# Capped attention and a gated two-layer block: the mix of keys through the PSUM bank of the values, and another order of a step

## The chip, the cores and the metric

The kernel runs on one core of a Trainium2 chip. The metric is the device time of one execution in microseconds (us). Engines are named as in the profile: PE (TensorE, matmuls), PEld (its weight loads), DVE (VectorE), ACT (ScalarE), POOL (GpSimd), SP (SyncE, which here only issues DMAs).

## The reference, cut to what matters

Batch 8, 12 heads, 448 positions, 64 channels a head. The attention's output, heads side by side (768 channels), goes into a block that mixes each position with the one before it.

```python
scores = cap * tanh(scale * q @ k.T / cap)
attn = exp(scores - max) / (sum(exp(scores - max)) + 1e-9)
x = attn @ v                      # heads side by side: 768 channels
xk = mu_k * x + (1 - mu_k) * x_prev     # x_prev: the position before, 0 at the first
xr = mu_r * x + (1 - mu_r) * x_prev
k = relu(xk @ w_k) ** 2                 # 768 -> 1024
out = sigmoid(xr @ w_r) * (k @ w_v)     # 768 -> 768
```

## The kernel before, in words

The first stage of the program walks over 48 pairs of heads (8 batches of 6 pairs; a pair fills the 128 partitions). Everything is kept transposed: scores have keys on partitions and queries along the free axis. A pair's scores come in four blocks of keys, S0 to S3 (`scores`, L182, the last of half size), each with three matmul passes on a high and a low part of q and k, so that the single-pass 32-bit format keeps its accuracy. ACT takes each block through tanh (L197) and exp (L207). PE multiplies the result by the values (`values`, V in the step, L216) into one PSUM bank, `pv`; the pool of these banks has two, used by turns, so that the value group two pairs later needs the bank again. DVE reduces each block's columns (`red`, L225), a DMA gathers the partial sums (`gather`, L230, tile `sq`), DVE adds and inverts them (`recip`, L234 to L238), and the reciprocals go out to DRAM (`rec_store`, L241) and come back spread over all partitions (`rec_load`, L246, tile `r`, one buffer, two DMAs).

`norm` (L250, DVE) multiplies the bank `pv` by `r` into the tile `X`, whose column 0 is zero, so that columns 0 to 447 are the previous positions and 1 to 448 the current ones. `mix_old` (L259, ACT) writes (1 - mu_k) times the previous positions, `mix_new` (L263, DVE) adds mu_k times the current ones in one instruction with two tensor inputs; `xk` (one buffer) is the result. POOL splits it into a high part (`x_high`, L70) and a low part (`x_low`, L80). POOL makes the same split of q and k for a later pair (`qk_high`, L70, and `qk_low`, L80). `x_store` (L275) writes X to DRAM for the second stage. The matmuls of the keys (K in the step, `kpart`, L298) run seven steps behind, 24 a step, into one of two banks; `relu` (L305, ACT) empties a bank and frees it, `k_store` (L311) sends it to DRAM from ACT's queue. Weights arrive as 64-bit numbers: one tile a step (two in some) is converted by five DVE instructions, the `f` entries (L357 to L365), with help of ACT (`weight_abs`, L337) and POOL (`weight_sum`, L372); the last of these instructions starts at 462.6 us.

The order of the instructions is written by hand in the string STEP (L47 to L49), and nothing reorders it: each engine, and SP's queue of DMAs, runs its own instructions in this order. In step i the loads are for pair i + 3, the q and k split for i + 2, scores, tanh, exp and red for pair i, V, gather, recip, rec_store and rec_load for i - 1, and norm, mix_old, mix_new, the split of xk and x_store for i - 2. A digit behind an entry is the block.

After the 48 pairs come seven steps of keys' matmuls alone, in which the converted weights of the second stage are loaded and split; and then the second stage: 28 chunks of 128 positions with the matmuls of L441.

Of the kernel before, what the change touches and what calls it, by code (L numbers as in the profile page):

```python
# [9 lines left out]
F32 = mybir.dt.float32  # L10
F32R = mybir.dt.float32r
AF = mybir.ActivationFunctionType
ALU = mybir.AluOpType
# [3 lines left out]
B, H, S, D = 8, 12, 448, 64  # L17
# [8 lines left out]
P = 128  # L26
# [17 lines left out]

STEP = """gather load_v weight_load more weight_low S0 S1 V S2 f f f f f weight_rest tanh0 exp0 red0 norm  # L47
weight_sum tanh1 recip rec_store exp1 red1 mix_old mix_new K qk_high qk_low x_high x_low tanh2 relu k_store
K exp2 red2 relu k_store S3 K K tanh3 exp3 red3 relu k_store weight_abs rec_load load_qk x_store weight_store"""  # L49


def f(ap):
# [3 lines left out]
class Body:  # L56
# [190 lines left out]
        self.R[i] = r  # L247

    def norm(self, i):
        self.nc.vector.tensor_mul(self.X[i % 2][:, 1:], self.PV.pop(i)[:, 0:S], self.R.pop(i))  # L250

    def mix_old(self, i):
        b, hp = i // NP, i % NP
        if hp == 0:
            xh = self.xkp[b % 2].tile([P, ND, S], F32R, name="xkh", tag="xkh")
            xl = self.xkp[b % 2].tile([P, ND, S], F32R, name="xkl", tag="xkl")
            self.XK[b] = (xh, xl)
        self.xk = self.up.tile([P, S], F32, name="xk", bufs=1)
        self.nc.scalar.mul(self.xk, self.X[i % 2][:, 0:S], self.om["k"][:, hp:hp + 1])  # L259

    def mix_new(self, i):
        hp = i % NP
        self.nc.vector.scalar_tensor_tensor(out=self.xk, in0=self.X[i % 2][:, 1:], scalar=self.mu["k"][:, hp:hp + 1],  # L263
                                            in1=self.xk, op0=ALU.mult, op1=ALU.add)

    def x_high(self, i, e="p"):
        self.copy(e, self.XK[i // NP][0][:, i % NP, :], self.xk)
# [193 lines left out]
    def step(self, i, KS):  # L461
# [6 lines left out]
        pair.update(dict.fromkeys("norm mix_old mix_new x_high x_low x_store".split(), i - 2))  # L468
        for op in STEP.split():
            j = pair.get(op)  # L470
# [180 lines left out]
```

## Time and profile before, and how to read it

| | us |
|---|---|
| runs of the kernel before | 1011.4, 1012.74 (median), 1013.64 |
| the profiled execution, its own time | 1016.09 |
| its span, first to last instruction | 1014.3 |
| PE busy in the span | 967.1 (95%) |
| DVE busy | 667.6 (66%) |
| ACT busy | 500.3 (49%) |
| POOL busy | 297.6 (29%) |

[...] A line such as `L263 DVE SCALAR_TENSOR_TENSOR xk<-x,mu_k,xk ... x48 | busy, mean` is one group: source line, engine, operation, tile written and tiles read, shapes, count, busy time in us, mean in ns, and behind the second bar the idle time of the engine before these instructions and what ended it. In the list of waits, `A <- B` means that A's engine stood idle until B was done. The chain follows the end of the program back from releaser to releaser. `SPq` and `ACTq` are the instruction queues of SP and ACT, in which DMAs are issued.

### The profile page before, as it was taken

The page shows a single profiled execution, that of the slowest core. Times are in us where ns is not written, and L with a number is a line of the kernel's source. Part 1 is how long each engine was busy: PE and PEld are TensorE (multiplying, and loading weights), DVE is VectorE, ACT ScalarE, POOL GpSimd, SP SyncE. Part 2 cuts the span into 40 slices and gives each one's busy share as a digit, 9 for nine tenths or more (in the row PEclk, how much of TensorE's full clock was granted, in tenths as well). Part 3 has the DMA queues.
Part 4 walks back from the last instruction along what each step waited for, and adds up shares of the span by engine and source line. Part 5 has one row for each costly group of instructions (what it writes and reads, how often), then busy time and mean ns, then how long its engine had stood idle before and what let it go on. Part 6 is the DMA issues. An engine that isn't in the chain of part 4 may idle for free.

```text
span 1014.3 us, 14549 instructions
## 1 busy us (share of the span) xinstructions
PE 967.1 (95%) x5280; PEld 781.6 (77%) x5280; DVE 667.6 (66%) x1202; ACT 500.3 (49%) x626; POOL 297.6 (29%) x267
## 2 busy tenths in 40 slices
PE   6678899999999999999999999999999999999997
PEld 3234566666666766766667899999999999999997
DVE  6999998777777777777556477455445544554550
ACT  6766678777788877777777212221122112211220
POOL 4555555554546454555442230000000000000000
PEclk8778999999999999999999999999999999999999
DMA  4555556666665666665552665233233323332320
GB/s 153 143 150 148 172 150 175 211 199 182 179 217 186 194 173 195 194 193 157 151 152 92 224 191 137 81 105 104 70 87 105 103 68 90 104 100 64 98 68 35
DMA packets 121249, 142.01 MB, mean 140 GB/s; under 512 B 19280, under 2 KB 100048, under 8 KB 121168
## 3 DMA queue, kind: packets, MB, share of 16 engines
q1 hardware_dynamic: 111952, 126.30, 43.5%
q10 hardware_dynamic: 9216, 14.68, 3.9%
q8 instruction: 44, 0.72, 0.3%
q14 instruction: 37, 0.30, 0.1%
HBM read 95.79 MB, written 42.40 MB: 136 GB/s over the span
## 4 chain that ended last, share of the span: by engine, by line
PE 61%; DVE 16%; DMA 14%; ACT 4%; issue 2%; SPq 1%; POOL 1%; ACTq 0%; DVEq 0%; POOLq 0%
PE pvv L441 22%; PE pr L441 17%; PE kps L298 10%; PE pv L216 7%; DMA sq<-r 6%; PE s L189 6%; DVE r L225 5%; DMA r<-rec_d 4%; ACT p L197 1%; DVE xk L263 1%; DMA rec_d<-rs 1%; DVE sr L234 1%; ACT p L207 1%; DVE wa L361 1%; SPq L230 1%
## 5 line engine op out<-in xcount | busy, mean ns | idle before, releaser
L225 DVE TRANSPOSE_TENSOR_REDUCE r<-p 128x28 f32<-128x896 f32 (+1 forms) x240 | 215.0, 905 | 44.5 <-ACT p L207 41.8
L197 ACT ACTIVATE p<-s,scl_t 128x896 f32<-128x896 f32 x192 | 173.1, 901 | 40.5 <-PE s L189 36.2
L207 ACT ACTIVATE p<-p,cap_t 128x896 f32<-128x896 f32 x192 | 182.5, 951 | 11.1 <-ACT ko L305 5.3
L74 ACT CAST xh<-t 128x768 fp32r<-128x768 f32 x27 | 22.7, 839 | 307.5 <-DVE t L424 307.5
L216 PE MATMUL pv<-p,rv 128*64 128x448 f32 x768 | 163.6, 570 | 0.0
L298 PE MATMUL kps<-xkh,wkh 128*128 128x448 f32 x384 | 147.4, 384 | 10.2 <-ACT ko L305 10.1
L456 DVE TENSOR_TENSOR o<-pvv,rsg 128x768 f32<-128x768 f32 (+1 forms) x29 | 27.0, 930 | 181.6 <-PE pvv L441 180.7
L298 PE MATMUL kps<-xkl,wkh 128*128 128x448 f32 x384 | 142.2, 370 | 0.0
L298 PE MATMUL kps<-xkh,wkl 128*128 128x448 f32 x384 | 142.1, 370 | 0.0
L216 PEld LDWEIGHTS pv<-p,rv 128*64 128x64 f32 x768 | 53.2, 143 | 89.5 <-issue 82.0
L441 PE MATMUL pvv<-wvh,kl 128*128 128x384 f32 x448 | 115.2, 335 | 0.0
L441 PE MATMUL pvv<-wvh,kh 128*128 128x384 f32 x448 | 115.2, 335 | 0.0
L441 PE MATMUL pvv<-wvl,kh 128*128 128x384 f32 x448 | 115.2, 335 | 0.0
L189 PE MATMUL s<-qkh 64*128 64x448 f32 (+1 forms) x336 | 85.6, 451 | 30.0 <-ACT p L197 25.0
L80 POOL TENSOR_TENSOR qkl<-rqk,qkh 128x960 fp32r<-128x960 f32 x47 | 105.9, 2253 | 3.9
L189 PEld LDWEIGHTS s<-qkh 64*128 64x128 f32 (+1 forms) x336 | 37.4, 191 | 87.4 <-ACT p L197 35.8
L298 PEld LDWEIGHTS kps<-xkh,wkh 128*128 128x128 f32 x384 | 73.2, 191 | 31.0 <-issue 13.1
L441 PE MATMUL pr<-wrh,xl 128*128 128x384 f32 x336 | 85.6, 336 | 0.8 <-DVE xl L432 0.8
L441 PE MATMUL pr<-wrh,xh 128*128 128x384 f32 x336 | 85.7, 336 | 0.1
L441 PE MATMUL pr<-wrl,xh 128*128 128x384 f32 x336 | 85.5, 335 | 0.0
L372 POOL TENSOR_TENSOR wsq<-wa,wsq 128x384 f32<-128x384 f32 x44 | 44.4, 1010 | 138.1 <-DVE wsq L365 138.1
L441 PEld LDWEIGHTS pvv<-wvl,kh 128*128 128x128 f32 x448 | 81.0, 188 | 0.0
(66 smaller groups left out, 1467.8 us busy)
## 6 DMA issues: line engine op xcount, KB each, us to landing
rqk<-qk SPq DMA_DIRECT2D x47, 480.0 KB
k_d<-ko ACTq DMA_DIRECT2D x64, 224.0 KB
kr<-k_d SPq DMA_DIRECT2D x28, 512.0 KB
rv<-v SPq DMA_DIRECT2D x48, 256.0 KB
x_d<-x SPq DMA_DIRECT2D x48, 224.5 KB
r<-rec_d SPq DMA_DIRECT2D x96, 112.0 KB
out<-o SPq DMA_DIRECT2D x27, 384.0 KB
xc<-x_d SPq DMA_DIRECT2D x24, 387.0 KB
```

The costliest lines, as they stand in the source:

```text
L74: self.nc.scalar.copy(out, x)
L80: {"p": self.nc.gpsimd, "v": self.nc.vector}[e].tensor_sub(*a)
L189: nc.tensor.matmul(s[:, h, 0:S], qk[a][p, k], qk[b][p, 0:S], start=(n == 0), stop=(n == 2))
L197: self.nc.scalar.activation(p32, self.S.pop((i, g))[:, :n, 0:S], AF.Tanh, scale=self.scl_t)
L207: self.nc.scalar.activation(p32, p32, AF.Exp, scale=1.0 if self.maxima else self.cap_t)
L216: nc.tensor.matmul(pv[p, 0:S], v[:, g, h, :], ph[:, h if g < 3 else 0, :], start=(g == 0), stop=(g == 3))
L225: self.nc.vector.tensor_reduce(out=out, in_=p32[p, h].rearrange("p h (b k) -> p (h b) k", k=32), axis=mybir.AxisListType.X, op=ALU.add, ap ...
L230: self.nc.sync.dma_start(self.sq[i % 2][:, q], self.r1[i % 2][32 * q:32 * q + 32])
L298: nc.tensor.matmul(self.kps[fc][:, 0:S], w, m[:, dc, :], start=first, stop=last)
L372: {"p": self.nc.gpsimd, "v": self.nc.vector}[e].tensor_add(sq, f(a), sq)
L441: self.nc.tensor.matmul(ps[:, m, 0:HN], a[:, c, :], w[:, c, m * HN:m * HN + HN], start=(c == 0 and part == 0), stop=(c == n - 1 and part = ...
L456: nc.vector.tensor_mul(o[:, q], pv[:, q, 0:HN], rs[:, q])
```

## The change

Three things change. The order of the step: `norm` moves from behind `red0` to behind `red1`, and with it `recip` and `rec_store` come behind `red1`; `mix_old` and `mix_new` move from ahead of the first K to behind `tanh2`; at the end of the step `load_qk` now stands ahead of `rec_load`. `mix_old` no longer writes the tile `xk` in SBUF; it overwrites the bank `pv` that norm has just read. `mix_new` reads that bank as its second input and writes `xk`, which is allocated there. The bank is given back after `mix_new`, no longer after `norm`.

```diff
-STEP = """gather load_v weight_load more weight_low S0 S1 V S2 f f f f f weight_rest tanh0 exp0 red0 norm
-weight_sum tanh1 recip rec_store exp1 red1 mix_old mix_new K qk_high qk_low x_high x_low tanh2 relu k_store
-K exp2 red2 relu k_store S3 K K tanh3 exp3 red3 relu k_store weight_abs rec_load load_qk x_store weight_store"""
+STEP = """gather load_v weight_load more weight_low S0 S1 V S2 f f f f f weight_rest tanh0 exp0 red0
+weight_sum tanh1 exp1 red1 norm recip rec_store K qk_high qk_low tanh2 mix_old mix_new x_high x_low relu k_store
+K exp2 red2 relu k_store S3 K K tanh3 exp3 red3 relu k_store weight_abs load_qk rec_load x_store weight_store"""
...
     def norm(self, i):
-        self.nc.vector.tensor_mul(self.X[i % 2][:, 1:], self.PV.pop(i)[:, 0:S], self.R.pop(i))
+        self.nc.vector.tensor_mul(self.X[i % 2][:, 1:], self.PV[i][:, 0:S], self.R.pop(i))
...
-        self.xk = self.up.tile([P, S], F32, name="xk", bufs=1)
-        self.nc.scalar.mul(self.xk, self.X[i % 2][:, 0:S], self.om["k"][:, hp:hp + 1])
+
+        self.xold = self.PV.pop(i)[:, 0:S]
+        self.nc.scalar.mul(self.xold, self.X[i % 2][:, 0:S], self.om["k"][:, hp:hp + 1])
...
     def mix_new(self, i):
         hp = i % NP
+        self.xk = self.up.tile([P, S], F32, name="xk", bufs=1)
         self.nc.vector.scalar_tensor_tensor(out=self.xk, in0=self.X[i % 2][:, 1:], scalar=self.mu["k"][:, hp:hp + 1],
-                                            in1=self.xk, op0=ALU.mult, op1=ALU.add)
+                                            in1=self.xold, op0=ALU.mult, op1=ALU.add)
```

## Rows read from the trace of the kernel before

**Rows 1.** Windows of 40 us: stretch, each engine's busy us, granted clock, DMA share.

```profile
core 0: us, PE busy (x) PEld busy (x) DVE busy (x) ACT busy (x) POOL busy (x), PEclk, DMA share, GB/s
...
40.00:80.00 40.00, 30.11 (x129) 13.17 (x127) 38.67 (x63) 27.67 (x35) 21.64 (x21) 0.78 0.54 164
...
440.00:480.00 40.00, 37.09 (x194) 25.86 (x195) 27.92 (x48) 29.89 (x38) 21.13 (x17) 0.96 0.59 180
...
480.00:520.00 40.00, 40.00 (x225) 27.52 (x225) 22.97 (x35) 29.25 (x36) 17.47 (x15) 1.00 0.52 145
```

**Rows 2.** Chain that ended last, V matmuls of chosen pairs: start us, us, what.

```profile
117.88 3.16 PE pv L216 x16
...
484.90 3.16 PE pv L216 x16
...
551.26 3.16 PE pv L216 x16
```

**Rows 3.** The same chain, one stall at 251 us.

```profile
230.48 5.81 DMA r<-rec_d
...
236.31 2.84 DMA sq<-r
...
250.79 0.53 ACT ko L305
...
251.36 4.19 PE kps L298 x12
```

**Rows 4.** Waits from 117 to 551 us: us in total, times, longest.

```profile
DVE sr L234 <- DMA sq<-r: 60.2, 29, 4.1
...
PE kps L298 <- ACT ko L305: 6.5, 3, 2.9
```

**Rows 5.** Groups of instructions by form, DVE and ACT.

```profile
L225 DVE TRANSPOSE_TENSOR_REDUCE r<-p 128x28 f32<-128x896 f32 x144 | 156.8, 1089 | 32.6 <-ACT p L207 32.4
...
L250 DVE TENSOR_TENSOR x<-pv,r 128x448 f32<-128x448 f32 x48 | 28.4, 591 | 5.4 <-DMA r<-rec_d 5.3
...
L207 ACT ACTIVATE p<-p,cap_t 128x896 f32<-128x896 f32 x144 | 150.3, 1044 | 9.6 <-ACT ko L305 5.3
...
L207 ACT ACTIVATE p<-p,cap_t 128x448 f32<-128x448 f32 x48 | 32.2, 670 | 1.6
...
L197 ACT ACTIVATE p<-s,scl_t 128x448 f32<-128x448 f32 x48 | 30.0, 624 | 11.2 <-PE s L189 6.9 <-ACT ko L305 3.6 <-DMA sq<-r 0.6
...
L259 ACT ACTIVATE xk<-x,om_k 128x448 f32<-128x448 f32 x48 | 32.0, 667 | 61.9 <-DVE x L250 61.7
```

**Rows 6.** Windows of L263 (mix_new) alone: stretch, its busy us (count).

```profile
30.00:155.00 125.00, 18.62 (x10) 0.86 0.53 154
...
155.00:575.00 420.00, 24.02 (x38) 0.99 0.59 177
```

**Rows 7.** Timeline, a step of the first stage, DVE and POOL: start us, us.

```profile
68.58 1.00 POOL L372 TENSOR_TENSOR wsq<-wa,wsq 128x384 f32<-128x384 f32 x1 [3.73 <-DVE wsq L365]
...
69.45 0.58 DVE L250 TENSOR_TENSOR x<-pv,r 128x448 f32<-128x448 f32 x1
...
69.96 0.59 DVE L234 TENSOR_REDUCE sr<-sq 32x28 f32<-32x448 f32 x1
...
71.07 1.06 DVE L225 TRANSPOSE_TENSOR_REDUCE r<-p 128x28 f32<-128x896 f32 x1
...
71.22 2.24 POOL L80 TENSOR_TENSOR qkl<-rqk,qkh 128x960 fp32r<-128x960 f32 x1
...
72.06 1.88 DVE L263 SCALAR_TENSOR_TENSOR xk<-x,mu_k,xk 128x448 f32<-128x448 f32 x1
```

**Rows 8.** Timeline, one step at 308 us, SP's queue.

```profile
308.56 0.34 SPq L241 DMA_DIRECT2D rec_d<-rs  x1
...
309.85 1.12 SPq L246 DMA_DIRECT2D r<-rec_d  x2
...
311.06 0.54 SPq L142 DMA_DIRECT2D rqk<-qk  x1
```

## The prediction, made before the changed kernel ran

> **What bounds the kernel now.** I read the stages first, by the windows, and then asked in each which wait ends last. There are three. From the start to about 118 us the PE works on scores and values alone and is not the bound: of 40 us it is busy for 30.1 at a granted clock of 0.78, while DVE is busy for 38.7 [rows 1]. DVE's own sequence is the step there. From 118 us the keys' matmuls come in and PE is busy almost throughout (40.0 of 40 in the best window), DVE for 23 to 28 [rows 1]. The chain gives the length of an undisturbed step: from 484.90 to 551.26 six value groups, so 66.36 / 6 = 11.06 us [rows 2]. The second half of the span is matmuls on loaded weights; the change touches nothing in it, and it only starts earlier or later.
>
> In the middle stage the value groups of 38 steps lie between 117.88 and 551.26: 433.4 us, where 38 x 11.06 = 420.3 would do [rows 2]. The excess is **13.1 us**, and most of it is three stalls in which PE waits for the relu that frees a bank of the keys, 6.5 us together, the longest 2.9 [rows 4], each with matmuls at the lower clock level behind it: twelve of them took 4.19 us after the stall at 251 us [rows 3], where the window with a stall shows a mean clock of 0.96 and one without 1.00 [rows 1]. The chain says why the relu was late. Back from it stand the gather of the row sums (236.31) and the load of the reciprocals (230.48, 5.81 us) [rows 3]: DVE's loop (reductions, gather DMA, recip, reductions again) takes a little longer than 11.06, DVE falls behind PE, and when the lag is used up PE pays it. DVE waits for the gather 29 times, 60.2 us, so 2.1 us each [rows 4], and the second reduction stands behind that wait. The lag grows by 13.1 / 38 = 0.34 us a step.
>
> **mix_new reads PSUM.** The old mix_new has two inputs in SBUF. It takes 18.62 / 10 = 1.86 us in the ten steps up to 155 us and 24.02 / 38 = 0.63 after that [rows 6]. In the first stage it starts at 72.06 while POOL's qk_low has run since 71.22, and it ends just after that one does [rows 7]: it is held up. The trace has no mix_new with an input in PSUM; its price lies between 0.59 (norm, same size, one input in PSUM [rows 5]) and 1.86 (still held up). Norm is the nearest, because it too has one operand in each memory and ran for 0.58 at 69.45, started while POOL's tensor add was under way [rows 7]; I take 0.63, the same operation unhindered. That is 1.23 less, in each of the seven held-up steps that precede the value group at 117.88: **8.6 us** of DVE's own time. The three held-up ones after that fall in steps that PE bounds; they count within the 13.1. [...]
>
> **mix_old writes PSUM.** The same ACTIVATE, 48 times, 0.667 us [rows 5]. No ACT write to PSUM is in the trace. The nearest rows are the same ACTIVATE into SBUF (0.667) and the tanh of this size, which reads PSUM (0.624) [rows 5]; a price up to the double-width exp's 1.04 cannot be excluded. I take 0.667, at no cost: ACT has 29 to 30 of 40 us busy [rows 1]. At 1.04, exp2 and with it red2 would be 0.4 late in the first stage, 2.6 us over seven steps.
>
> **norm behind red1, mix_old behind tanh2.** Nothing is added; the order changes on three engines. On DVE red1 (1.09 [rows 5]) now runs before norm and recip. The gather gets 1.09 us more before recip asks for it, so the loop through the gather shrinks by 1.09 against a growth of 0.34: in the middle stage the lag no longer builds up. I count 11 of the 13.1 us as gone, and leave 2 for a late DMA here and there. On ACT, tanh2 no longer stands behind norm. Mix_old, the relu and exp2 still do, and norm comes later by red1 (1.09) while mix_old no longer pushes tanh2 in front of exp2 (about 1.0): the relu moves by 0.1. In the first stage exp2 and exp3 now follow norm more closely than red2 and red3 want them. From norm's end DVE does recip (71.07 - 69.96 = 1.11 [rows 7]), mix_new 0.63 and red2 1.09, 2.83 in all; ACT does mix_old 0.67, exp2 1.04, tanh3 0.62, exp3 0.67, 3.0 [rows 5], and about 0.1 for the hand-over. So red3 waits 0.3 a step: **2.1 us lost** over seven. Whoever is behind mix_new (POOL's x_high and x_low) has its result some 0.6 sooner.
>
> **PV is held to mix_new instead of norm**, recip and mix_new longer: 1.11 + 0.63 = 1.7 us. Behind it waits the value group two pairs on. It starts at the end of the scores of the next step, and the wait stays hidden as long as DVE is not behind.
>
> **rec_load behind load_qk on SP.** The loads of r wait for rec_store to land, 309.85 - 308.56 = 1.3 us, and load_qk stood behind them, at 311.06 [rows 8]. It is now issued inside that wait, some 1.9 us sooner; x_store, the weight store and the next gather lose nothing. What is exposed is r itself: its two loads queue behind 480 KB. Norm wants r 11.06 - 1.11 - 0.59 = 9.4 us after recip ends, since recip then follows norm in the next step. Store and loads took at worst 1.3 + 0.5 + 5.81 = 7.6 [rows 3, 8]; one transfer more is about 2 (load_qk's lead), so 9.6 at worst, seldom late. I cost it at nothing, covered by that slack; where it is late, norm, mix_old and the relu are late by as much, a few tenths.
>
> **Sum.** First stage 8.6 - 2.1 = 6.5; middle 11.0; together 17.5 us less. The profiled execution took 1016.09 us (span 1014.3, 1.8 around it) and would take 998.6. The median of the runs, 1012.74, lies 3.35 lower; the forecast against it is **995 us**. Bounds: the first stage between -2 (mix_new still held up, red3 late) and +9, the middle between 0 and 13.
>
> **Rivals.**
> (1) The lag stays. If what makes DVE late is DMA arriving late rather than the place of red1, r behind load_qk eats what the gather gains. For it: the chain at 230 us goes through both DMAs [rows 3]. Against: the gather's wait is seen 29 times [rows 4]. Then only the first stage pays: 1012.7 - 6.5 = 1006.
> (2) mix_new stays held up by POOL in spite of its PSUM input. Then the first stage gives -2 and the middle 11: 1012.7 + 2 - 11 = 1004. Against it stands norm's row. [...]
> (3) Slower: ACT becomes the loop. exp1 -> red1 -> norm -> mix_old puts 1.09 + 0.59 of DVE's work into ACT's sequence. Before, norm hung on exp0 and was done under tanh1 and exp1. tanh2 fills 1.0 of the 1.7 only if PE has delivered its scores by then. If it has not, ACT's step grows by 1.7. ACT's busy 29.89 of 40 is 8.3 per step [rows 1], and 1.7 more makes 10.0, below 11.06; the point where it decides is 1.1 us of other idle time a step on ACT (DMA issues of the key store, waits for scores). At an idle time of 1.6 the step would be 11.5: 38 x 0.44 = 17 us over the 420.3, 3.6 more than today's 13.1, and in the first stage ACT would eat the gain. That is about 1016.
> (4) Both gains fail: 1013.
>
> **Chances.** Forecast 0.60, rival (1) 0.20, (2) 0.08, (3) 0.08, (4) 0.04. The range 987 to 1008 holds the forecast with the ends of its terms (6.5 and 11 up to 9 and 13, with a little for PE's clock when the stalls go) and the rivals (1) and (2). A measurement of this kernel tells about 0.2%, 2 us, from no change. Faster: 0.60 + 0.20 + 0.08 = 0.88; same: 0.04; slower: 0.08.
>
> **What would show it.** Right: mix_new at about 0.6 in all 48 steps; DVE's wait for the gather near half of 60 us; no relu wait of over 2 us on PE between 117 and 551, and 11.06 us a step; the first value group of the middle stage some 6 us sooner. Wrong: mix_new of 1.9 in the first ten steps; norm waiting for r in many steps; PE's value group waiting for mix_new; ACT without idle time between exp1 and the relu's end while PE waits for it.

## The result, and the profile after

Over four runs each on one chip, the kernel took 1012.07 us before (1010.97 to 1013.64) and 1002.42 us after (1000.24 to 1004.32). The ratio is 0.9903, with a 95% interval of 0.9877 to 0.9929: some 10 us faster, where 17.5 were forecast. The profiled executions took 1016.09 and 1003.25 us, with spans of 1014.3 and 1001.4. Before lay 4.0 above its median there and after 0.8, so the traces differ by 12.9 us, and 3.2 of these belong to the two executions, not to the change.

I cut the span at two value groups: the **first stage** runs to the one that opens the middle stage, the **middle** is the 38 steps behind it, the **rest** goes from there to the end.

| profiled execution, us | before | after | less | forecast |
|---|---|---|---|---|
| first stage | 117.8 | 112.7 | 5.1 | 6.5 |
| middle, 38 steps | 433.4 | 422.8 | 10.6 | 11.0 |
| rest | 463.1 | 466.0 | -2.9 | 0 |

The chain that ended last (start us, us, what) shows the first two. Between these rows lie 37 steps, (524.49 - 112.72) / 37 = 11.13 us each, where an undisturbed step takes 11.06 and the mean before was 433.4 / 38 = 11.40.

```profile
112.72 3.16 PE pv L216 x16
...
479.93 3.16 PE pv L216 x16
...
524.49 3.16 PE pv L216 x16
```

The windows that answer to [rows 1], in the same columns: DVE is still nearly full in the first stage (37.15 of 40), and the window that held a stall (37.09 of PE busy, TensorE's granted clock 0.96 of its full speed) now has none.

```profile
40.00:80.00 40.00, 28.02 (x138) 12.39 (x134) 37.15 (x64) 27.32 (x35) 22.85 (x23) 0.84 0.56 167
440.00:480.00 40.00, 39.93 (x222) 28.17 (x222) 26.79 (x43) 30.78 (x40) 19.14 (x17) 1.00 0.55 172
480.00:520.00 40.00, 39.94 (x218) 26.60 (x217) 24.27 (x37) 31.01 (x38) 17.58 (x14) 1.00 0.43 132
```

The waits from 110 to 545 us (total, times, longest). Both rows of [rows 4] are gone: the list has neither a wait of DVE for the gather nor one of PE for a relu. What DVE waits for in their place is ACT's exp; with PE full, 39.9 of 40 us above, that costs nothing that shows.

```profile
DVE r L225 <- ACT p L207: 80.9, 81, 2.7
...
ACT pv L260 <- DVE x L250: 17.2, 39, 3.1
...
POOL qkh L70 <- DMA rqk<-qk: 9.3, 5, 2.0
```

The groups that answer to [rows 5], DVE's and then ACT's (shapes, count, busy us, mean ns, idle before), and mix_new in the two stretches of [rows 6].

```profile
L225 DVE TRANSPOSE_TENSOR_REDUCE r<-p 128x28 f32<-128x896 f32 x144 | 158.6, 1109 | 62.2 <-ACT p L207 61.9
...
L265 DVE SCALAR_TENSOR_TENSOR xk<-x,mu_k,pv 128x448 f32<-128x448 f32 x48 | 30.6, 638 | 1.9 <-ACT pv L260 1.9
L250 DVE TENSOR_TENSOR x<-pv,r 128x448 f32<-128x448 f32 x48 | 28.3, 589 | 6.6 <-DMA r<-rec_d 6.6
...
L260 ACT ACTIVATE pv<-x,om_k 128x448 f32<-128x448 f32 x48 | 30.6, 638 | 40.0 <-DVE x L250 40.0
...
30.00:155.00 125.00, 7.11 (x11) 0.88 0.53 163
155.00:575.00 420.00, 23.49 (x37) 1.00 0.58 185
```

mix_new takes 7.11 / 11 = 0.65 us in the early stretch, where it took 1.86, and 0.64 over all. The timeline of the stage that [rows 7] showed (start us, us) has it beside POOL's qk_low, and not held up:

```profile
67.41 0.59 DVE L250 TENSOR_TENSOR x<-pv,r 128x448 f32<-128x448 f32 x1
...
68.19 2.23 POOL L80 TENSOR_TENSOR qkl<-rqk,qkh 128x960 fp32r<-128x960 f32 x1
...
68.75 0.63 ACT L260 ACTIVATE pv<-x,om_k 128x448 f32<-128x448 f32 x1
...
69.50 0.68 DVE L265 SCALAR_TENSOR_TENSOR xk<-x,mu_k,pv 128x448 f32<-128x448 f32 x1 [0.40 <-ACT pv L260]
...
70.38 1.11 DVE L225 TRANSPOSE_TENSOR_REDUCE r<-p 128x28 f32<-128x896 f32 x1 [0.20 <-ACT p L207]
```

The two brackets are new in this step: DVE now waits for mix_old and for an exp inside the stage that it bounds. From the start to 112 us it waits 1.2 us for mix_old (3 times) and 3.4 for exp (6 times), where before it waited 3.1 for exp (2 times, to 117 us). And at the turn to the second half PE waits four times for the first inputs, 0.84 + 0.85 + 1.07 + 0.17 = 2.93 us, where before it waited 0.65 + 0.17 = 0.82. First after, then before:

```profile
584.40 0.62 PE L443 MATMUL pr<-wrh,xh 128*128 128x384 f32 x2 [0.84 <-POOL xh L70]
...
586.22 0.62 PE L443 MATMUL pr<-wrh,xl 128*128 128x384 f32 x2 [0.85 <-DVE xl L434]
...
601.44 0.62 PE L443 MATMUL pr<-wrh,xh 128*128 128x384 f32 x2 [1.07 <-ACT xh L74]
```

```profile
600.17 0.62 PE L441 MATMUL pr<-wrh,xl 128*128 128x384 f32 x2 [0.65 <-DVE xl L432]
```

### The profile page after: what moved, and what is told of

The parts are those of the page before. It is cut to its first block, busy times and chain, and to the rows that moved or that the text cites. A ratio compares the mean times of both kernels' runs of the same rounds, so it can differ in the third digit from the quotient of the medians.

```text
span 1001.4 us, 14566 instructions
## 1 busy us (share of the span) xinstructions
PE 959.3 (96%) x5280; PEld 776.2 (78%) x5280; DVE 665.4 (66%) x1202; ACT 499.1 (50%) x626; POOL 296.8 (30%) x267
## 4 chain that ended last, share of the span: by engine, by line
PE 73%; DVE 8%; ACT 7%; DMA 6%; issue 2%; SPq 2%; POOL 0%; ACTq 0%; DVEq 0%; POOLq 0%
PE pvv L443 22%; PE pr L443 17%; PE kps L300 15%; PE pv L216 10%; PE s L189 9%; ACT p L207 3%; ACT p L197 2%; DMA rv<-v 2%; DVE r L225 2%; DMA wst<-w_d 1%; SPq L230 1%; DVE x L250 1%; ACT pv L260 1%; DVE wa L363 1%; DVE wt L359 1%
## 5 line engine op out<-in xcount | busy, mean ns | idle before, releaser
L225 DVE TRANSPOSE_TENSOR_REDUCE r<-p 128x28 f32<-128x896 f32 (+1 forms) x240 | 220.1, 922 | 87.7 <-ACT p L207 82.8
L300 PEld LDWEIGHTS kps<-xkh,wkh 128*128 128x128 f32 x384 | 72.0, 188 | 23.9 <-issue 13.1
L443 PEld LDWEIGHTS pvv<-wvh,kl 128*128 128x128 f32 x448 | 81.0, 188 | 0.0
```

Of the source, the lines that this page charges most:

```text
L225: self.nc.vector.tensor_reduce(out=out, in_=p32[p, h].rearrange("p h (b k) -> p (h b) k", k=32), axis=mybir.AxisListType.X, op=ALU.add, ap ...
L300: nc.tensor.matmul(self.kps[fc][:, 0:S], w, m[:, dc, :], start=first, stop=last)
L443: self.nc.tensor.matmul(ps[:, m, 0:HN], a[:, c, :], w[:, c, m * HN:m * HN + HN], start=(c == 0 and part == 0), stop=(c == n - 1 and part = ...
```

## The experiments

The question was which part of the change brought which part of the gain. The forecast laid the middle to red1 standing ahead of recip, and the swap of load_qk and rec_load at nothing. The table gives every kernel's three parts, from its profiled execution, with DVE's wait for the gather in the middle (row `DVE sr <- DMA sq<-r`), and the time against before on the same chip. The times are from several chips, on which the median of before goes from 1012.1 to 1016.4 us, so kernels are compared by the ratio.

| kernel | first stage | middle | rest | wait for the gather, us (times) | us | ratio, 95% interval |
|---|---|---|---|---|---|---|
| before | 117.8 | 433.4 | 463.1 | 60.2 (29) | | 1 |
| before again (e4) | 118.0 | 434.4 | 464.3 | 59.8 (30) | 1018.5, one run | |
| after | 112.7 | 422.8 | 466.0 | none | 1002.4 | 0.9903 (0.9877 to 0.9929) |
| e1 all order, mix in SBUF | 114.7 | 424.3 | 466.9 | none | 1009.3 | 0.9929 (0.9904 to 0.9954) |
| e2 PSUM alone | 112.6 | 430.2 | 462.6 | 81.6 (35) | 1007.3 | 0.9908 (0.9881 to 0.9936) |
| e3 swap alone | 117.7 | 421.8 | 462.9 | 1.9 (3) | 1005.0 | 0.9894 (0.9873 to 0.9916) |
| e5 norm, recip behind red1 alone | 120.3 | 442.0 | 465.3 | 40.5 (27) | 1029.4, one run | |
| e6 mix behind tanh2 alone | 116.3 | 439.3 | 464.1 | 80.6 (33) | 1021.6, one run | |
| e7 after, inputs of the second half sooner | 113.9 | 422.7 | 467.4 | 0.4 (1) | 1005.1 | 0.9887 (0.9866 to 0.9909) |
| e8 after without swap | 114.2 | 430.0 | 466.6 | 59.8 (32) | 1009.8 | 0.9925 (0.9896 to 0.9954) |
| e9 PSUM and swap | 112.3 | 421.0 | 462.9 | 0.2 (1) | 998.0 | 0.9817 (0.9788 to 0.9846) |
| e10 before, load_qk behind gather | 118.2 | 431.3 | 463.3 | 40.2 (26) | 1014.7 | 0.9994 (0.9971 to 1.0018) |
| e11 PSUM, load_qk behind gather | 112.9 | 427.2 | 464.1 | 41.7 (29) | 998.4 | 0.983 (0.9809 to 0.9852) |
| e12 PSUM, swap, mix moved | 108.1 | 421.0 | 463.5 | 1.8 (4) | 995.0 | 0.981 (0.9783 to 0.9838) |

### The change in two halves, and the kernel before once more (e1, e2, e4)

e1 takes the new order of the step whole and leaves the mix in SBUF. e2 takes only the mix through PSUM.

```diff
 e1, against before: all three lines of STEP as in the change
-weight_sum tanh1 recip rec_store exp1 red1 mix_old mix_new K qk_high qk_low x_high x_low tanh2 relu k_store
+weight_sum tanh1 exp1 red1 norm recip rec_store K qk_high qk_low tanh2 mix_old mix_new x_high x_low relu k_store
...
 e2, against before
-        self.nc.scalar.mul(self.xk, self.X[i % 2][:, 0:S], self.om["k"][:, hp:hp + 1])
+        self.xold = self.PV.pop(i)[:, 0:S]
+        self.nc.scalar.mul(self.xold, self.X[i % 2][:, 0:S], self.om["k"][:, hp:hp + 1])
...
-                                            in1=self.xk, op0=ALU.mult, op1=ALU.add)
+                                            in1=self.xold, op0=ALU.mult, op1=ALU.add)
```

> The new order of the step, with mix_old writing the tile xk in SBUF and mix_new reading it there, as before. Theory (the order cures the middle stage, PSUM the first): the relu stalls between 117 and 551 us are gone, 11.06 us a step, about 10 us less there; mix_new is held up by POOL in the first steps, 1.2 us each, so that the first value group of the middle stage comes no earlier than before (117 to 119 us); the turn to the second half gives back 2 to 3 us. In all 1004 to 1007 us. Rival (PSUM is what matters): the stalls stay, 1012 us.

> mix_old writes the bank of the values and mix_new reads it, with the old order of the step. Theory: mix_new takes 0.63 us in all 48 steps; the first value group of the middle stage comes 6 to 8 us sooner than 117.8, more than in the changed kernel since red2 and red3 don't wait for ACT; the stalls of the middle stage stay, some 10 to 13 us over 11.06 a step. In all 1005 to 1007 us. Rival (mix_new in PSUM is also what freed the middle stage): the stalls are gone, below 1000 us.

> The kernel before, unchanged, profiled once more. Theory: the stalls of the middle stage vary from one execution to another with the DMAs' times; the profiled execution of before (1016.1 against a median of 1012.1) had one more or a longer one, so this one shows an excess over 11.06 us a step of 8 to 13 us, and the first value group of the middle stage again at 117.8 within 0.5. Rival: the excess is the same 13 us each time, and the difference lies elsewhere.

The PSUM half alone gains 5.2 us in the first stage (117.8 to 112.6; 6 to 8 were expected) and 3.2 in the middle; DVE's wait for the gather does not get shorter, it grows to 81.6. The order alone, with the swap in it, gains 9.1 in the middle, and its gather wait is gone, but the rest is 3.8 longer. It also gains 3.1 in the first stage, where nothing was expected. e4, the kernel before in another execution, shows the noise of such a reading: 434.4 against 433.4 in the middle, with its stalls at other places, and so no smaller excess than the first one had, against its theory. Both executions lay 3 to 4 us above the median of their chip, so a typical middle of before may be shorter, and the 3.2 of e2 may be no more than that; the 9 to 12 of e1, e3 and after are well outside it.

### The swap by itself, and the change without it (e3, e8)

```diff
 e3, against before (e8 undoes this in after)
-K exp2 red2 relu k_store S3 K K tanh3 exp3 red3 relu k_store weight_abs rec_load load_qk x_store weight_store"""
+K exp2 red2 relu k_store S3 K K tanh3 exp3 red3 relu k_store weight_abs load_qk rec_load x_store weight_store"""
```

> The kernel before with load_qk ahead of rec_load, nothing else. Theory: no difference by itself beyond 2 us, 1010 to 1014; POOL's wait for rqk shrinks from 53 us to under 20. Rival (DMAs that come late make DVE's lag): the stalls of the middle stage shrink, 1003 to 1007 us.

> The changed kernel with rec_load again ahead of load_qk. Theory after the first runs (load_qk in the DMA queue ahead of the gather made DVE late, and its move alone cures the middle stage): without the move only red1's 1.09 us help the gather; the gather lands again 5.5 us after its issue (4.3 in the changed kernel), DVE waits for it again, and 4 to 9 us of excess over 11.06 us a step come back: 1004 to 1008 us. Rival (red1 ahead of norm and recip is enough, the two cures are alternatives): the excess stays under 4 us and the time at 1001 to 1004 us.

Two words in another order take the middle from 433.4 to 421.8, within 1.5 of 38 undisturbed steps, although red1 stands where it stood, and the swap alone (0.9894) is as fast as the whole change (0.9903) within the intervals. This was the rival of e3's expectation, not its theory. Everything but the swap, with red1 ahead of recip, leaves 430.0. The profiled execution of e8 was the slowest of its six, 2.8 above their median, so a little of that may be its own; by the runs alone, 0.9925 (0.9896 to 0.9954), e8 is not told apart from after. The gather's wait tells them apart: 59.8 us against none. The waits of e3 and of e8 from 117 to 535 us:

```profile
DVE sr L234 <- DMA sq<-r: 1.9, 3, 1.0
```

```profile
POOL qkh L70 <- DMA rqk<-qk: 67.8, 28, 6.0
DVE sr L234 <- DMA sq<-r: 59.8, 32, 3.5
```

Where it comes from stands in one step's timeline. In before, load_qk's 480 KB go out at 311.06 [rows 8] and the gather's four DMAs from 312.64, behind reductions that end at 310.02 + 2.29 = 312.31. DVE reduces the next pair's first block, does norm, and then stands 1.84 us for the gather, until 318.06:

```profile
310.02 2.29 DVE L225 TRANSPOSE_TENSOR_REDUCE r<-p 128x28 f32<-128x896 f32 x3
...
314.60 1.11 DVE L225 TRANSPOSE_TENSOR_REDUCE r<-p 128x28 f32<-128x896 f32 x1
...
318.06 0.61 DVE L234 TENSOR_REDUCE sr<-sq 32x28 f32<-32x448 f32 x1 [1.84 <-DMA sq<-r]
```

SP's queue of before, the row of that gather (start us, us):

```profile
312.64 2.45 SPq L230 DMA_DIRECT2D sq<-r  x4
```

In e3 load_qk goes out 0.42 us behind rec_store, in the time in which the loads of r wait for that store to land anyway; the gather starts 3.7 us behind load_qk instead of 1.6 (SP's queue, start us, us):

```profile
301.42 0.34 SPq L241 DMA_DIRECT2D rec_d<-rs  x1
301.84 0.34 SPq L142 DMA_DIRECT2D rqk<-qk  x1
302.71 1.12 SPq L246 DMA_DIRECT2D r<-rec_d  x2
...
305.56 2.45 SPq L230 DMA_DIRECT2D sq<-r  x4
```

Read off the records of the traces for steps 10 to 40, from the gather's first issue to the landing of its last part, the mean is 5.6 us in before and 4.0 in e3; from the end of the step's last reduction to that landing, 6.04 and 3.38. So the loop's DMA part is some 2.7 us a step shorter, against a lag that grew by 0.34 a step. This second figure sorts all fourteen kernels: it is 3.3 to 4.4 us in the six with the swap, whose middle takes 421.0 to 424.3, and 5.7 to 7.1 in the eight without it, with 427.2 to 442.0. The largest, 7.1, is that of e8, which has red1 ahead of recip. Counted from its own first issue, the gather behind the 480 KB landed 1.6 us later (5.6 against 4.0); r behind the same 480 KB, below, was not later. What in the queue makes the one wait and not the other is not shown.

The other thing to see in e3 is that r, which now queues behind the 480 KB, is not later: from the issue of rec_store to its landing 5.6 us, against 5.9 in before. And e3 has 28 held-up mix_news of 48 (over 1 us) where before has 10: POOL's split of q and k, which no longer waits for its load (2.8 us in the stretch, 47.8 before), now falls on mix_new in the middle too (38.58 us for 38 of them from 155 to 575 us, 1.02 each, where before took 0.63 [rows 6]). There PE is the bound and it costs nothing that shows.

### The two moves by themselves (e5, e6)

```diff
 e5, against before: red0 ends the line above; norm, recip and rec_store behind red1, the mix stays ahead of K
-weight_sum tanh1 recip rec_store exp1 red1 mix_old mix_new K qk_high qk_low x_high x_low tanh2 relu k_store
+weight_sum tanh1 exp1 red1 norm recip rec_store mix_old mix_new K qk_high qk_low x_high x_low tanh2 relu k_store
 e6, against before: mix_old and mix_new behind tanh2, norm and recip stay
-weight_sum tanh1 recip rec_store exp1 red1 mix_old mix_new K qk_high qk_low x_high x_low tanh2 relu k_store
+weight_sum tanh1 recip rec_store exp1 red1 K qk_high qk_low tanh2 mix_old mix_new x_high x_low relu k_store
```

> The kernel before with norm, recip and rec_store behind red1, nothing else (mix_old and mix_new behind them, ahead of tanh2, in SBUF). If red1 in front of recip cures the middle stage: excess over 11.06 us a step under 4 us. If only the move of load_qk does: 9 to 14 us. The first stage: ACT's mix_old now stands in front of tanh2 and waits for a later norm, so tanh2 and the scores come 1 us later there; first value group of the middle stage 118 to 124 us.

> The kernel before with mix_old and mix_new behind tanh2, norm and recip where they were. In the middle stage nothing that the gather waits for has moved: excess 10 to 14 us, as before. If ACT's wait of 62 us for norm was a cause of the stalls, under 8 us. First value group of the middle stage at 115 to 118 us.

e5 is what the forecast took for the cure of the middle. The gather's wait does fall, to 40.5, but the kernel is the slowest of all: 1029.4, where the runs of before on that chip went from 1012.6 to 1020.8, and a middle of 442.0. ACT now waits for norm 36 times (30.5 us in 20 times before), and in e5 tanh2 stands behind that wait:

```profile
ACT xk L259 <- DVE x L250: 71.0, 36, 4.5
...
DVE sr L234 <- DMA sq<-r: 40.5, 27, 3.6
```

Of the two excesses that were expected (under 4, or 9 to 14) neither came: 442.0 is 21.7 over 38 undisturbed steps. By these waits, red1 ahead of recip gives the gather time and takes it again from the path through norm, mix_old and exp2; no run separates the two. e6, at 1021.6 in one run, is not clearly outside before's runs; its first stage is 1.5 shorter and its middle longer, with a gather wait of 80.6. Why that wait grew was not tried.

### PSUM and swap without any move (e9), and the one move that pays (e12)

e9 is the kernel after with before's STEP and only load_qk and rec_load exchanged. e12 is the kernel after with norm, recip and rec_store back behind red0:

```diff
 e9, against after
-STEP = """gather load_v weight_load more weight_low S0 S1 V S2 f f f f f weight_rest tanh0 exp0 red0
-weight_sum tanh1 exp1 red1 norm recip rec_store K qk_high qk_low tanh2 mix_old mix_new x_high x_low relu k_store
+STEP = """gather load_v weight_load more weight_low S0 S1 V S2 f f f f f weight_rest tanh0 exp0 red0 norm
+weight_sum tanh1 recip rec_store exp1 red1 mix_old mix_new K qk_high qk_low x_high x_low tanh2 relu k_store
 e12, against after
-STEP = """gather load_v weight_load more weight_low S0 S1 V S2 f f f f f weight_rest tanh0 exp0 red0
-weight_sum tanh1 exp1 red1 norm recip rec_store K qk_high qk_low tanh2 mix_old mix_new x_high x_low relu k_store
+STEP = """gather load_v weight_load more weight_low S0 S1 V S2 f f f f f weight_rest tanh0 exp0 red0 norm
+weight_sum tanh1 recip rec_store exp1 red1 K qk_high qk_low tanh2 mix_old mix_new x_high x_low relu k_store
```

> The old order of norm, recip, mix_old and mix_new, with mix_old and mix_new through the bank of the values and load_qk ahead of rec_load. Theory (these two carry the gain, the moves of norm and mix nothing): first value group of the middle stage at 112.6, excess there 1.5 to 2.5 us, and the turn to the second half without the 2.4 us that the changed kernel lost: 997 to 1000 us, 2 to 5 us below the changed kernel. Rival (the moves of norm and mix are needed too): 1003 to 1007 us.

> The changed kernel with norm, recip and rec_store back behind red0; mix_old and mix_new stay behind tanh2, in the bank of the values, and load_qk stays ahead of rec_load. Theory (norm and recip behind red1 put the stores of the reciprocals 2 us later against PE, and that is what the changed kernel pays at the turn and every sixth step): the turn as in the version with the old order, time from the keys' last matmul to the end 415 to 416 us instead of 417.8, excess of the middle stage under 1.5 us, 996 to 999 us. Rival (the move of the mix behind tanh2 costs it): 1001 to 1004 us.

e9 has the first stage of e2 and the middle of e3, and beats the whole change: 0.9817 against 0.9903, intervals apart. From e2 it differs by the swap alone, and is faster with the intervals apart as well (0.9908 there). So norm and recip behind red1, together with the mix behind tanh2, cost more than they bring. e12 divides the two. Its first stage is 4.6 us shorter than that of after, its rest 2.5 shorter, and it has the lowest time of the study: 995.0 us, 0.981 (0.9783 to 0.9838). Against e9 the profile puts it 4.2 us ahead in the first stage, but the two intervals overlap, and the runs alone do not separate them. Chain and waits (117 to 535 us) of e12; the two value groups are 38 steps apart, 421.01 / 38 = 11.08:

```profile
108.16 3.16 PE pv L216 x16
...
529.17 3.16 PE pv L216 x16
```

```profile
DVE sr L234 <- DMA sq<-r: 1.8, 4, 0.8
```

In the first stage DVE of e12 runs this, without a gap: norm at 65.37, recip, red1, mix_new, and red2 and red3 behind it as one row of three.

```profile
65.37 0.59 DVE L250 TENSOR_TENSOR x<-pv,r 128x448 f32<-128x448 f32 x1
65.88 0.59 DVE L234 TENSOR_REDUCE sr<-sq 32x28 f32<-32x448 f32 x1
...
66.98 1.06 DVE L225 TRANSPOSE_TENSOR_REDUCE r<-p 128x28 f32<-128x896 f32 x1
67.98 0.63 DVE L265 SCALAR_TENSOR_TENSOR xk<-x,mu_k,pv 128x448 f32<-128x448 f32 x1
68.54 2.29 DVE L225 TRANSPOSE_TENSOR_REDUCE r<-p 128x28 f32<-128x896 f32 x3
```

Here mix_old (ACT, 65.99 to 66.63 in that step) is written while recip and red1 run. In after, norm comes behind red1, so that only recip lies between norm and mix_new, and DVE pays the hand-over to ACT and back: 0.40 + 0.20 us in the step shown above. Over the whole first stage DVE waits 4.6 us for mix_old and exp in after, and 1.3 for exp alone in e12. That is 3.3 of the 4.6 by which the stages differ; the rest is not traced to a wait.

### Where load_qk may stand (e10, e11)

```diff
 e10, against before (e11: the same in e9)
-STEP = """gather load_v weight_load more weight_low S0 S1 V S2 f f f f f weight_rest tanh0 exp0 red0 norm
+STEP = """gather load_qk load_v weight_load more weight_low S0 S1 V S2 f f f f f weight_rest tanh0 exp0 red0 norm
...
-K exp2 red2 relu k_store S3 K K tanh3 exp3 red3 relu k_store weight_abs rec_load load_qk x_store weight_store"""
+K exp2 red2 relu k_store S3 K K tanh3 exp3 red3 relu k_store weight_abs rec_load x_store weight_store"""
```

> The kernel before with load_qk moved behind the gather, to the start of the step; rec_load stays where it was, so nothing is put ahead of it. Theory (480 KB in the queue between rec_load and the gather is what made the gather late): the gather lands 4 us or less after its first issue instead of 5.6, DVE's wait for it falls from 60 us to under 15, the excess of the middle stage to under 3 us, 1003 to 1006 us. Rival (it was SP's wait in front of rec_load that load_qk fills): the gather stays at 5 us or more and most of the excess stays, 1010 us or more.

> The same move of load_qk with mix_old and mix_new through the bank of the values and the old order of norm and mix. Theory: as the version with load_qk ahead of rec_load, 996 to 999 us; no excess in the middle stage (under 2 us). Rival: load_v and the weight load now queue behind 480 KB and PE waits for values, over 1000 us.

With load_qk behind it, the gather lands 3.8 us after its first issue (5.6 before). Yet DVE's wait falls only to 40.2 us, where under 15 was expected, and nothing is gained, 0.9994 (0.9971 to 1.0018). SP's queue shows why: rec_store goes out soon behind the three big loads of the step, lands late, and the loads of r wait for it 230.91 - 226.58 = 4.3 us, where [rows 8] had 1.3 (in the mean of steps 10 to 40, 3.4 against 1.4). Everything behind them goes later, the gather too: its issue follows the last reduction by 1.9 us in the mean (0.4 in before), so that it lands 5.7 us behind that reduction, little sooner than the 6.0 of before.

```profile
226.58 0.34 SPq L241 DMA_DIRECT2D rec_d<-rs  x1
230.91 1.13 SPq L246 DMA_DIRECT2D r<-rec_d  x2
...
233.23 2.45 SPq L230 DMA_DIRECT2D sq<-r  x4
235.77 0.53 SPq L142 DMA_DIRECT2D rqk<-qk  x1
```

So it is not the gather alone that must be kept clear, it is the chain rec_store, r, gather. The run also speaks against another reading of the swap, that it pays because POOL gets q and k sooner: in the middle of e10 POOL never waits for their load (47.8 us in before), and the middle still takes 431.3. Of the three places tried, only the one inside rec_store's own landing leaves both ends alone. With the PSUM mix the picture is less plain: e11 runs at 0.983 (0.9809 to 0.9852), as fast as e9 within the intervals. Its profiled execution took 1006.4 us, the slowest of its six (the others 997.9 to 1000.5), so its middle of 427.2 is not typical. That execution has the late gather of e10, 5.8 us behind the last reduction. Why the place behind the gather does no harm in most of e11's runs stays open, and with it whether the chain must be kept clear once the mix is in PSUM.

### The turn to the second half (e7)

```diff
 e7, against after: the first inputs of the second half are loaded a step earlier
-                if i == NPAIR + 4:
+                if i == NPAIR + 3:
```

> The changed kernel with the preparation of the second half's first chunk one step earlier, ahead of three of the weight splits. Theory (the changed kernel lost 2.4 us at the turn because the last norm, and with it DVE's row of splits and preparation, comes later against PE): PE's two waits of 0.85 us at the first chunk go, and the second half begins with the keys' last matmul; 1.5 us or so less, 999 to 1002 us. Rival (the loads of the weights set the turn): the wait moves to the value weights or to the second chunk, no gain or a loss of up to 5 us.

PE no longer waits at the first chunk, and waits at the second instead, 3.41 us in one place. The rest is 467.4 against 466.0, and the ratio, 0.9887 (0.9866 to 0.9909), is not told apart from that of after.

```profile
602.96 0.80 PE L443 MATMUL pr<-wrh,xh 128*128 128x384 f32 x2 [3.41 <-ACT xh L74]
```

The rest column sorts the kernels by one thing. The five with norm and recip behind red1 (after, e1, e5, e7, e8) have 465.3 to 467.4, mean 466.4; the nine without it (before, e2, e3, e4, e6, e9 to e12) have 462.6 to 464.3, mean 463.4. So that move costs some 3 us at the turn in the mean, whatever else is changed. A possible reason is read from the timelines: the last pairs' rec_store goes out later against the value groups. In before the second-last goes out at 555.5, 5.3 us ahead of the last value group (560.8), in after at 541.8, 3.3 ahead of it (545.1); it is 3.3 in all five and 5.3 in all nine. That the loss runs through this delay was not tested by itself, and it does not fall in one place: in e1 it lies ahead of the keys' last matmul (41.9 us from the last value group, 38.0 in before), in after behind it (417.8 us from there to the end, 415.5 in before).

## Why the prediction was right or wrong

**Sign and range** hold: faster at 0.88, and 1002.4 lies in 987 to 1008. The forecast of 995 was 7.4 too low; it set out from the median 1012.74 of three runs, which the fourth made 1012.07. By its own sum, 17.5 us against the 12.9 of the traces, 1.3 are missing in the first stage, 0.4 in the middle and 2.9 in the rest. The other 3.2, down to the medians' 9.65, come from the two profiled executions: the forecast carried the distance of before to its median (3.35) over to the new kernel, which lay only 0.8 above its own. Before's middle may have held more stalls than a typical one, but that is not shown, as e4 had the same.

**mix_new reads PSUM: right.** 0.64 us against 0.63 forecast, in all 48 steps; rival (2) is out. With its second input in PSUM it took 638 ns in the mean, against 24.02 / 38 = 632 unhindered from SBUF [rows 6]. With both inputs in SBUF 10 of 48 were held up in before and 28 in e3; those of before took 1.56 to 1.93 us, each beside POOL's qk_low for 1.08 us or more. In after 11 ran beside qk_low from start to end and took 0.63 to 0.68.

**What that is worth in the first stage: too much.** The step "1.23 less, in each of the seven held-up steps" took all of DVE's time as path. e2, which does that part alone, gives 5.2, and e9 against e3 5.4. Part of the 1.23 has become a wait for ACT: over the first stage DVE waits 4.3 us for exp in e9 and 2.4 in e3, which is 1.9 of the 3.2 that are missing. ACT's waits tell why: from 60 us to the end of the stage it stands 11.3 us (4 times) for norm in e9, with tanh2 behind it, and 4.9 (2 times) in e12, where the mix is behind tanh2 and the first stage is 9.7 us shorter than before.

**mix_old writes PSUM: right**, and a little better than nothing: 638 ns against 667.

**norm behind red1: the 2.1 us lost was mis-sized.** It costs 4.6 in the first stage (after against e12), and DVE waits for mix_old too, not only for exp3. The 4.2 that mix behind tanh2 brings (e12 against e9) had no term of its own. 8.6 - 2.1 stands against 5.4 + 4.2 - 4.6 = 5.0, so the stage came out close by errors that cancel, which is luck.

**The middle: right size, wrong cause.** This is the step that failed: "The gather gets 1.09 us more before recip asks for it, so the loop through the gather shrinks by 1.09". e5, which does that alone, is slower than before; e8, which does it with all else but the swap, keeps 59.8 us of gather waits. That the size fits, 10.6 against 11.0, is luck too: the term was taken from the excess of 13.1, and any cure of the excess would have given it. What removes the waits is load_qk's new place, the step of which I wrote "I cost it at nothing, covered by that slack". I asked whether r would be late behind the 480 KB, and did not ask what they had stood in front of until then: the next DMA behind [rows 8] that a loop waits for is the gather, at 312.64. "x_store, the weight store and the next gather lose nothing" was true and half of the answer, since the gather gains. [rows 4] showed a wait on a DMA, and I answered it with more time for that DMA before asking why it landed late. Rival (1) had the right suspicion, "DMA arriving late rather than the place of red1", and the wrong sign for the swap. One reading of the stalls was off as well: not each of the three had matmuls at the lower clock level behind it. The granted clock is 0.66 from 251 to 256 us and from 456 to 461, but 1.00 from 387 to 391, behind the stall that ends at 387.52.

**The second half, "it only starts earlier or later": wrong by 2.9 us.** The five kernels with norm and recip behind red1 all pay there, so the place of the last pairs' norm and stores is part of the turn; by which path is not shown.

**Rival (3), ACT as the loop**, did not come in the whole change; by the waits it did in e5, where the mix stays ahead of tanh2 (ACT waits 71.0 us for norm, and PE 12.0 for a relu, 6.5 in before).

Of the tests that the forecast named, mix_new at 0.6 and no relu wait came true; the gather's wait went to none, not to half, which already spoke for another cause than 1.09 us more time; the first value group came 5.1 us sooner, not 6, and a step took 11.13 us, not 11.06.

## What to carry to other kernels

When an engine waits for a small DMA, read what stands ahead of it on its queue before reordering the engines (here 480 KB, with which the gather took 5.6 us to land, without them 4.0); a large transfer that nobody waited for soon paid here in a time in which the queue waits anyway, behind a store whose landing the next load needs (two words, 0.9894). Time taken off the busiest engine counted here only as far as the neighbour that feeds it had its results ready: move a producer behind its input and ahead of its consumer, with other work between on both sides, and price the move on each engine. Test a change of several parts by its parts: here one part cost 0.0093 of the ratio (0.9903 - 0.981), some 9 us that the others hid, and without it the kernel (e12) had the lowest time, though e9 and e11 are not told apart from it.

## What was not expected of the hardware

- 480 KB put on the queue directly ahead of the loads of r did not make r later (5.6 us from rec_store against 5.9), while the same 480 KB ahead of the gather made it land 1.6 us later. What in the transfers makes the difference was not tried.
- The order of the DMAs alone changed how long the packets took. From 120 to 540 us the packets of SP's queue (packets, MB, share of 16 engines) took 53.6% in before and 49.1% in e3, for the same data to within 1%; after, e3, e9 and e12, all with the swap, have 48.7 to 49.5%, e8 without it 54.1%. It is not this that the middle gains by: e10, which gains nothing, has 47.8%.

```profile
q1 hardware_dynamic: 39410, 64.09, 53.6%
```

```profile
q1 hardware_dynamic: 39792, 64.52, 49.1%
```

- The same ACTIVATE of 128x448 took 638 ns into PSUM (after) and 667 into SBUF (before), over 48 instructions each: 29 ns less.
